# RWKV attention and a squared-ReLU MLP: the four w_in loads on ScalarE's DMA queue

## The chip, the cores and the metric

The kernel runs on one core of one Trainium2 chip. The core has TensorE (PE, with the weight load PEld beside it), VectorE (DVE), ScalarE (ACT), GpSimd (POOL) and SyncE (SP), and 16 DMA engines that move what the queues of the issuing engines hand them. The metric is the device time of one execution in microseconds (us); lower is better. In three runs the kernel took 182.17, 182.38 and 182.93 us, a median of 182.38 us.

## The reference

The first half is a linear attention with a decaying state (RWKV-6), for 4 batches, 8 heads, 768 tokens and 48 values per head. The second half is an MLP over the 3072 tokens, from 384 to 2048 values and back, with a squared ReLU between. All inputs and the output are float32.

```python
for t in range(S):                       # per batch b and head h
    cur = outer(u * k[t], v[t])
    y[t] = r[t] @ (state + cur)
    state = w[t][:, None] * state + outer(k[t], v[t])
x = y laid out as (4 * 768, 8 * 48)
h = maximum(x @ w_in, 0.0)               # w_in: 384 x 2048
out = (h * h) @ w_out                    # w_out: 2048 x 384
```

## The kernel before

The 3072 tokens are cut into 12 steps of 256 tokens, three steps to a batch. Each step has an attention part and an MLP part. Inside a step the tokens stand in two chunks of 128 rows.

The attention part of step s loads w, k, r and v (384 KB each: 128 partitions, 8 heads, two neighbouring tokens of 48 floats, so 384 bytes in one piece). POOL or DVE multiplies pairs of w (`ww_`), ACT takes the logarithm (`lw_`), PE sums it along the tokens (`cum_`), ACT takes the exponential (`exp_`, and `ac_` for the decay of a whole chunk). POOL makes the products of k and w (`kw_`, line 290), of r and w (`rw_`, line 286) and of k and u (`ku_`, `qp_`). DVE multiplies r and k by the decay (`rd_.s.0` makes rdec, line 358; `rd_.s.1` makes kdec, line 361). PE transposes both (`tr_`), and ACT or DVE copies the transposes out of PSUM (`rkt_`). PE makes the products of r and k (`p_`, line 420), the update of the state (`su_`, from v and kdec), the two parts of y (`y_`, `yc_`), and transposes y (`yt_`). ACT casts v (`v_`, and `vs_` in another order of rows). `vq_` (POOL or DVE, line 316) is the part of the token itself, which DVE adds to y (`ysb_`).

The MLP part runs in groups. `m1_.s.g` is one group of the first product (line 536), followed by the ReLU on ACT or DVE (`rl_`) and the square (`sq_`). `m2_` is the second product (line 561), `os_` scales it and `store` writes it out. Group g of `m1_` covers columns 256 g to 256 g + 255 of w_in, so it needs block g // 2 of four.

The weights are loaded once. Each of the four blocks of w_in (128 x 3 x 512 floats, 768 KB, pieces of 2 KB) is loaded into one of four staging buffers (`w_st`, `load_wi`) and cast to bf16 (`cast.i.g`, line 200). The four blocks of w_out (`load_wo`, `cast.o.g`) then use the same four staging buffers, so a w_out load waits for a cast of w_in. Blocks 1 and 0 of w_in are cast by ACT, 2 and 3 by POOL.

The order of the work is not left to a scheduler. The string ORDER lists all operations, and each engine does its own in this order; a letter behind `=` names the engine of an operation that can stand on several (A for ACT, V for DVE, G for POOL). All loads, stores and DMA transposes are issued by SP, also in this order. The entries `warm_.n.b` are n products of zeros on PE whose result nobody uses. Before the first m1, PE has step 0 and most of steps 1 and 2 of the attention in its order; the first m1 groups are 3 and 2 (block 1), then 1 and 0 (block 0), then 5 and 4 (block 2).

SP issues, at the start: w, k, r, u of step 0, w 1, v 0, k 1, r 1, w 2, v 1, r 2, k 2, then w_in blocks 1, 0 and 2, v 2, w_in block 3, w_out block 0, w 3, and so on. Eight completion semaphores are used in turn, so a DMA also waits, before it is issued, for the one eight places ahead of it.

Of the kernel before, what the change touches and what calls it, by code (L numbers as in the profile page):

```python
# [27 lines left out]
m1_.0.5:0 v_.2=A xt_.1=V qp_.2=G sn_.1.1 m1_.0.4:1 rl_.0.5=A p_.2.1:1 su_.2:b sq_.0.0=A rl_.0.4=V ld.2.o
m1_.1.4:0 cast.i.3=G ts_.2.0=V pm_.2.1 m1_.1.5:1 rl_.1.4=A q_.2 sn_.2.0 m1_.1.3:0 rl_.1.5=A ld.3.o vs_.2.1=G
vs_.2.0=A yc_.2.0:0 yc_.2.1:0 rl_.1.3=V m1_.1.6:1 cast.o.0=G qs_.2=A m1_.1.0:0 ld.3.k rl_.1.6=V sq_.0.2=A  # L30
y_.2:0 rl_.1.0=V m1_.1.1:1 vq_.2=G m1_.1.7:0 rl_.1.1=V ld.3.v m2_.0.1.0:0 sq_.1.2=A rl_.1.7=V sq_.0.1=A
cast.o.1=G m1_.1.2:1 rl_.1.2=A ysb_.2=V m1_.0.7:0 ld.4.w ww_.3=G yt_.2:1 rl_.0.7=V m1_.0.6:1 xt_.2=V m2_.0.1.1
sq_.1.1=A rl_.0.6=V ld.5.w m1_.2.6:0 cast.o.2=G lw_.3 sq_.1.0=A rl_.2.6=A cum_.3:1 sq_.1.3=A rw_.3=G al_.3
ld.5.r m2_.0.0.0:1 m1_.2.7:1 m2_.0.0.1 cast.o.3=V exp_.3 sq_.0.3=A ld.4.k rd_.3.0 kw_.3=G m1_.2.1:0 rl_.2.7=A
ac_.3 m2_.0.1.2 m2_.0.0.2 rl_.2.1=V ku_.3=G m2_.0.0.3 rd_.3.1 ld.4.v m2_.0.1.3 vs_.3.0=A m1_.2.0:1 os_.0.1=V
qp_.3=G ld.5.v m1_.2.3:0 os_.0.0=V rl_.2.0=V tr_.3.1:0 rl_.2.3=A tr_.3.0:1 rkt_.3.1=V v_.3=A ld.4.r m1_.2.4:1
ww_.4=G rkt_.3.0=V m2_.1.0.0:0 rl_.2.4=A q_.3 ww_.5=G p_.3.1:0 vs_.3.1=A ld.6.k su_.3:1 pm_.3.1 p_.3.0:m
m2_.1.0.1 ts_.3.0=A lw_.4 sn_.3.0 ld.5.k pm_.3.0 m2_.1.0.2 qs_.3=A m2_.1.1.0:1 sq_.2.0=A vq_.3=G ts_.3.1=V
m2_.1.0.3 ld.6.w cum_.4:0 m2_.1.1.1 ku_.4=G ac_.4 al_.4 store.0.1 m1_.2.5:0 os_.1.0=A v_.5=A yc_.3.1:1 y_.3:1
lw_.5 kw_.4=G m1_.2.2:1 ld.6.r ysb_.3=V rl_.2.5=A m2_.1.1.2 exp_.4 sn_.3.1 rl_.2.2=V yt_.3:0 rw_.4=G cum_.5:1  # L40
xt_.3=V m2_.1.1.3 vs_.4.0=A ac_.5 sq_.2.1=A qp_.4=G al_.5 m1_.3.0:0 rd_.4.1 v_.4=A m1_.3.3:1 rd_.4.0 dtr_.4.1
m2_.2.0.0:0 rl_.3.0=A rw_.5=G rl_.3.3=A m2_.2.0.1 os_.1.1=V exp_.5 q_.4 dtr_.4.0 su_.4:0 sq_.2.2=A m1_.3.4:0
kw_.5=G rd_.5.0 ww_.6=G m2_.2.1.0:1 rl_.3.4=A ts_.4.0=V sq_.2.3=A m1_.3.5:1 vs_.4.1=A rd_.5.1 sn_.4.0
m2_.2.1.1 store.1.0 ts_.4.1=V rl_.3.5=V ku_.5=G m1_.3.6:0 store.1.1 m2_.2.1.2 qs_.4=A ld.7.w ld.6.v rw_.6=G
p_.4.1:1 rl_.3.6=A p_.4.0:0 pm_.4.1 pm_.4.0 m2_.2.1.3 lw_.6 vq_.4=G m1_.3.1:1 m1_.3.2:0 rl_.3.1=A su_.5:1
dtr_.5.1 dtr_.5.0 vs_.5.1=G sq_.3.0=A rl_.3.2=V yc_.4.0:0 yc_.4.1:0 sn_.4.1 y_.4:0 os_.2.1=V sq_.3.1=A
m1_.3.7:1 ysb_.4=V ld.7.v m2_.2.0.2 rl_.3.7=A ld.8.w kw_.6=G vs_.5.0=G yt_.4:1 ld.7.k sq_.3.3=A m2_.2.0.3
xt_.4=V cum_.6:0 al_.6 m1_.4.4:0 qp_.5=G os_.2.0=A ac_.6 m1_.4.7:1 ts_.5.0=V exp_.6 rl_.4.4=V m2_.3.0.0:1
rl_.4.7=A rd_.6.1 m1_.4.6:0 rd_.6.0 m2_.3.0.1 dtr_.6.1 m2_.3.1.0:0 ku_.6=G qp_.6=G sq_.3.2=A rl_.4.6=A q_.5
dtr_.6.0 p_.5.0:1 p_.5.1:0 vs_.6.0=A m1_.4.5:1 sn_.5.0 m2_.3.0.2 qs_.5=G rl_.4.5=A pm_.5.1 pm_.5.0 vq_.5=G  # L50
m1_.4.1:0 m1_.4.3:1 rl_.4.3=A store.2.1 ld.8.v m2_.3.0.3 rl_.4.1=V ld.8.k v_.6=A ww_.7=G y_.5:0 q_.6 os_.3.0=A
ld.7.r m1_.4.0:1 store.0.0 ld.9.k ww_.8=G yc_.5.0:0 qs_.6=A su_.6:1 yc_.5.1:0 ysb_.5=V vs_.6.1=A ts_.6.0=V
m1_.4.2:0 ld.8.r m2_.3.1.1 rl_.4.0=V yt_.5:1 xt_.5=V sn_.6.0 lw_.7 vq_.6=G rl_.4.2=A p_.6.0:0 m2_.3.1.2
sq_.4.3=A store.2.0 pm_.6.0 m1_.5.2:1 ku_.7=G m1_.5.6:0 ts_.6.1=V yc_.6.1:0 sq_.4.0=A rl_.5.2=A p_.6.1:1
rl_.5.6=A m2_.3.1.3 kw_.7=G pm_.6.1 sq_.4.2=A m1_.5.4:1 rw_.7=G m1_.5.3:0 os_.3.1=V rl_.5.4=A y_.6:0 sn_.6.1
rl_.5.3=A cum_.7:1 kw_.8=G ysb_.6=V al_.7 m2_.4.0.0:1 vs_.7.1=A m1_.5.7:1 m1_.5.5:0 v_.7=G dyt_.6 sq_.4.1=A
rl_.5.7=V qp_.7=G rl_.5.5=V m2_.4.1.0:0 exp_.7 ld.9.w ld.9.v m2_.4.0.1 ac_.7 rd_.7.0 sq_.5.1=A m2_.4.0.2
ku_.8=G rd_.7.1 sq_.5.3=A dtr_.7.0 m2_.4.0.3 m1_.5.0:1 lw_.8 m1_.5.1:0 rw_.8=G rl_.5.0=V su_.7:0 q_.7
rl_.5.1=A cum_.8:1 dtr_.7.1 m1_.6.3:1 qs_.7=A m1_.6.5:0 rl_.6.3=V ld.10.w qp_.8=G ac_.8 sq_.5.0=A m2_.4.1.1
os_.4.0=V ts_.7.0=V ld.11.w sn_.7.0 m1_.6.4:1 rl_.6.5=A al_.8 ww_.9=G m2_.4.1.2 ld.9.r rl_.6.4=V exp_.8  # L60
store.3.0 m2_.5.1.0:1 sq_.5.2=A rd_.8.1 ts_.7.1=V sn_.7.1 m1_.6.0:0 vs_.7.0=G vs_.9.1=A rd_.8.0 m2_.4.1.3
m2_.5.1.1 kw_.9=G rl_.6.0=A dtr_.8.0 p_.7.1:0 v_.8=A p_.7.0:1 vq_.7=G pm_.7.1 m1_.6.1:1 m2_.5.1.2 rl_.6.1=A
pm_.7.0 ku_.9=G m2_.5.1.3 sq_.6.0=A lw_.9 m1_.6.6:0 dtr_.8.1 store.3.1 q_.8 yc_.7.0:0 v_.9=A yc_.7.1:0
rl_.6.6=V rw_.9=G su_.8:1 y_.7:0 os_.5.1=A ts_.8.0=V m1_.6.2:1 ysb_.7=V os_.4.1=A cum_.9:1 m1_.6.7:0 al_.9
dyt_.7 m2_.5.0.0:1 rl_.6.2=V exp_.9 ww_.10=G rl_.6.7=V m2_.5.0.1 ac_.9 ld.10.r rd_.9.1 sq_.6.1=A sq_.6.2=A
sn_.8.0 qp_.9=G ld.10.k qs_.8=G store.4.1 m2_.5.0.2 ld.10.v rd_.9.0 m2_.5.0.3 m2_.6.1.0:0 vs_.8.1=G sq_.6.3=A
dtr_.9.0 vs_.8.0=A p_.8.0:m p_.8.1:0 pm_.8.0 su_.9:1 m2_.6.1.1 ts_.9.0=A pm_.8.1 m2_.6.1.2 lw_.10 m1_.7.4:0
rw_.10=G os_.5.0=V m1_.7.0:1 rl_.7.4=V sn_.9.0 vq_.8=G yc_.8.1:0 dtr_.9.1 yc_.8.0:0 rl_.7.0=V y_.8:0 m1_.7.1:0
q_.9 rl_.7.1=A ts_.9.1=V m2_.6.1.3 kw_.10=G ysb_.8=V m1_.7.7:1 sq_.7.0=A ww_.11=G cum_.10:1 dyt_.8 rl_.7.7=V
m1_.7.5:0 qs_.9=A al_.10 m2_.6.0.0:1 v_.10=G rl_.7.5=A m1_.7.2:1 exp_.10 ld.11.k vs_.9.0=G m2_.6.0.1 lw_.11  # L70
rd_.10.0 rd_.10.1 m1_.7.3:0 rl_.7.2=A vq_.9=G ac_.10 m2_.6.0.2 os_.6.1=A rl_.7.3=A vs_.10.0=A store.6.1
m1_.7.6:1 store.5.1 ku_.10=G m2_.6.0.3 vs_.10.1=A ld.11.r sn_.9.1 rl_.7.6=V m1_.8.5:0 dtr_.10.0 p_.9.1:0
rl_.8.5=A p_.9.0:1 qp_.10=G pm_.9.1 m1_.8.3:1 m2_.7.0.0:0 rl_.8.3=A pm_.9.0 m1_.8.4:0 sq_.7.1=A m1_.8.2:1
os_.6.0=A y_.9:0 sq_.7.3=A rl_.8.2=V yc_.9.1:0 rw_.11=G su_.10:1 m2_.7.1.0:1 sq_.7.2=A ts_.10.0=V ysb_.9=V
m2_.7.1.1 rl_.8.4=A ku_.11=G q_.10 m1_.8.7:1 dyt_.9 m1_.8.1:0 rl_.8.7=V cum_.11:0 dtr_.10.1 kw_.11=G sn_.10.0
rl_.8.1=A m2_.7.1.2 al_.11 m1_.8.0:1 exp_.11 ld.11.v qs_.10=G ts_.10.1=V sn_.10.1 vq_.10=G m1_.8.6:0 rl_.8.0=A
store.6.0 rd_.11.0 m2_.7.1.3 rl_.8.6=A rd_.11.1 m1_.9.4:1 sq_.8.0=A ac_.11 dtr_.11.0 m1_.9.1:0 qp_.11=G
rl_.9.4=V sq_.8.2=A m2_.7.0.1 os_.7.1=V p_.10.1:1 sq_.8.1=A p_.10.0:0 pm_.10.1 store.5.0 dtr_.11.1 store.7.1
m1_.9.0:1 v_.11=G pm_.10.0 vs_.11.1=G m2_.8.1.0:1 rl_.9.0=A rl_.9.1=A m2_.8.1.1 sq_.8.3=V m1_.9.5:1 m2_.7.0.2
m2_.7.0.3 os_.7.0=A yc_.10.0:1 yc_.10.1:1 rl_.9.5=V su_.11:0 y_.10:1 m1_.9.2:0 ysb_.10=V m1_.9.6:1 rl_.9.2=A  # L80
ts_.11.0=V dyt_.10 m2_.8.0.0:0 rl_.9.6=V sn_.11.0 m1_.9.3:0 q_.11 m2_.8.1.2 rl_.9.3=A yc_.11.0:1 vs_.11.0=A
p_.11.1:0 yc_.11.1:1 p_.11.0:m m2_.8.0.1 pm_.11.0 m2_.8.0.2 pm_.11.1 sq_.9.1=A m2_.8.0.3 m2_.8.1.3 qs_.11=A
# [549 lines left out]
```

## Time and profile before

| What | Value |
|---|---|
| Runs | 182.17, 182.38, 182.93 us |
| Span of the profiled execution | 182.2 us |
| PE busy | 171.8 us (94%) |
| DVE, ACT, POOL busy | 130.0, 132.7, 122.7 us |
| Loads of w_in | 4 of 768 KB, median 11.1 us from issue to landing |
| Loads of w, k, r, v | 48 of 384 KB, medians 5.3 to 5.9 us |
| Hardware DMA queue | 79184 packets, 35.46 MB |

The page gives the profiled execution by its span alone, from the first to the last instruction; the runs are the device's own time, and their median lies 0.2 us above that span.

How to read it: busy times of engines run beside each other and do not add up. A row of the timeline has the start in us, the time it took, the engine, the line, the operation, the tile written, the tile read and the count; brackets give the idle time of the engine before it and what ended that. SPq is SP as it issues DMAs: the time in such a row is the issue, and the data land later. The DMA rows give that second time, from issue to landing.

### The profile page before, as it was taken

The numbers are of one execution on the slowest core, as the hardware profiler recorded it, in microseconds if no ns is written. First come the engines' busy times: TensorE is split into PE (matmuls) and PEld (weight loads), VectorE is DVE, ScalarE is ACT, GpSimd is POOL, SyncE is SP. The second block draws the span as 40 slices with busy tenths as digits, with TensorE's granted clock in tenths as the row PEclk, the third lists the DMA queues.
The fourth block names the chain that finished last, engine by engine and source line by source line (L and its number), as shares of the span: only waits on it lengthen the run. The fifth ranks groups of instructions, "written<-read, shape, count | busy, mean of one in ns | idle before, by whom it ended". The sixth has DMA issues, their size and how long they took to land.

```text
span 182.2 us, 5695 instructions
## 1 busy us (share of the span) xinstructions
PE 171.8 (94%) x2385; PEld 123.4 (68%) x2385; DVE 130.0 (71%) x195; ACT 132.7 (73%) x235; POOL 122.7 (67%) x140
## 2 busy tenths in 40 slices
...
DMA packets 79208, 35.81 MB, mean 197 GB/s; under 512 B 72400, under 2 KB 77648, under 8 KB 79184
## 3 DMA queue, kind: packets, MB, share of 16 engines
q1 hardware_dynamic: 79184, 35.46, 85.9%
...
## 4 chain that ended last, share of the span: by engine, by line
PE 75%; SPq 10%; DMA 8%; ACT 4%; issue 1%; DVE 1%; ACTq 0%
PE bk L561 32%; PE m L536 32%; SPq L178 8%; DMA w_st<-in_moe_w_in_dram 5%; PE att L420 3%; DMA rT<-rdec_buf 2%; PE att L483 2%; PE att L493 2%; PE att L446 1%; ACT gt L545 1%; PE att L326 1%; ACT wi_sb L200 1%; PE bk L516 1%; SPq L188 1%; SPq L205 1%
## 5 line engine op out<-in xcount | busy, mean ns | idle before, releaser
L536 PE MATMUL m<-xT,wi_sb 128*128 128x256 bf16 x576 | 74.0, 273 | 1.3 <-ACT gt L545 1.2
L561 PE MATMUL bk<-wo_sb,gt 128*128 128x384 bf16 x384 | 71.9, 326 | 0.0
L536 PEld LDWEIGHTS <-wi_sb 128*128 128x128 bf16 x576 | 54.8, 98 | 13.0 <-issue 0.9
L561 PEld LDWEIGHTS <-gt 128*128 128x128 bf16 x384 | 36.9, 98 | 19.2
L545 ACT ACTIVATE gt<-m 128x512 f16<-128x512 f32 x56 | 33.0, 595 | 22.3 <-PE m L536 21.9
L553 ACT ACTIVATE gt<-gt 128x1024 bf16<-128x1024 f16 x42 | 43.3, 1051 | 1.4 <-DVE gt L547 1.1
L547 DVE TENSOR_SCALAR gt<-m 128x512 f16<-128x512 f32 x40 | 27.0, 686 | 9.6 <-PE m L536 9.3
L434 DVE TENSOR_TENSOR pmT<-att,mask 128x1024 bf16<-128x1024 f32 x20 | 23.9, 1218 | 4.5 <-PE att L420 4.5
L297 POOL TENSOR_TENSOR ku<-k_raw,u_bc 128x768 f32<-128x768 f32 x12 | 21.8, 1819 | 0.2 <-DMA u_bc<-in_u_dram 0.2
L302 POOL TENSOR_TENSOR ku<-ku,r_raw 128x768 f32<-128x768 f32 x11 | 20.7, 1881 | 0.2
L316 POOL TENSOR_TENSOR ku<-v_sh,qs 128x768 f32<-128x768 bf16 x11 | 16.3, 1479 | 4.9 <-ACT qs L277 4.8
L277 ACT CAST v_sh<-v_raw 64x384 bf16<-64x384 f32 x34 | 17.3, 508 | 0.4
L290 POOL TENSOR_TENSOR k_raw<-k_raw,w_raw 128x384 f32<-128x384 f32 x12 | 12.2, 1013 | 6.4 <-DMA k_raw<-in_k_dram 6.3
L286 POOL TENSOR_TENSOR r_raw<-r_raw,w_raw 128x384 f32<-128x384 f32 x12 | 12.0, 1000 | 6.4 <-DMA r_raw<-in_r_dram 6.4
L504 DVE TENSOR_TENSOR y_sb<-att,ku 128x768 bf16<-128x768 f32 x12 | 11.4, 953 | 5.5 <-issue 1.6
L461 POOL TENSOR_TENSOR S<-t_state,ac_buf 128x192 bf16<-128x192 f32 x20 | 10.2, 512 | 6.4 <-DVE t_state L456 3.4
L361 DVE TENSOR_TENSOR kdec_buf<-k_raw,att 128x768 bf16<-128x768 f32 x12 | 11.4, 949 | 3.4 <-ACT att L340 2.8
L358 DVE TENSOR_TENSOR rdec_buf<-r_raw,att 128x384 bf16<-128x384 f32 x24 | 12.1, 547 | 2.2 <-ACT att L340 1.1
L340 ACT ACTIVATE att<-att 128x768 f32<-128x768 f32 x12 | 9.6, 798 | 3.1 <-PE att L328 1.9
L568 ACT ACTIVATE o_sb<-bk 128x384 f32<-128x384 f32 x13 | 6.3, 485 | 7.4 <-PE bk L561 7.3
L307 DVE TENSOR_REDUCE q<-ku 128x16 f32<-128x768 f32 x12 | 11.3, 943 | 0.0
L578 PE MATMUL att<-warm 128*128 128x512 bf16 x27 | 9.1, 492 | 1.2 <-DVE half_ones L228 1.2
...
## 6 DMA issues: line engine op xcount, KB each, us to landing
w_raw<-in_w_dram SPq DMA_DIRECT2D x12, 384.0 KB, 5.3
k_raw<-in_k_dram SPq DMA_DIRECT2D x12, 384.0 KB, 5.9
r_raw<-in_r_dram SPq DMA_DIRECT2D x12, 384.0 KB, 5.7
v_raw<-in_v_dram SPq DMA_DIRECT2D x12, 384.0 KB, 5.8
...
w_st<-in_moe_w_in_dram SPq DMA_DIRECT2D x4, 768.0 KB, 11.1
w_st<-in_moe_w_out_dram SPq DMA_DIRECT2D x4, 768.0 KB, 9.3
rT<-rdec_buf SPq DMA_TRANSPOSE x16, 4.1
```

The costliest lines, as they stand in the source:

```text
L178: nc.sync.dma_start(out=t[:, hs, at:at + 2, :].rearrange("p h j d -> p h (j d)"), in_=src[b, hs, i * T:(i + 1) * T, :].rearrange("h (p j) ...
L277: copy(out[j * Q:(j + 1) * Q, c], src[c * Q:(c + 1) * Q, :, j])
L290: tensor_mul("kw_", s, h)(raw["k", s][:, hs, 0, :], raw["k", s][:, hs, 1, :], raw["w", s][:, hs, 1, :])
L297: tensor_mul("ku_", s, h)(tiles["ku", s][:, hs], raw["k", s][:, hs, 1:3, :], u_bc[:, hs, None, :].to_broadcast([C, n, 2, D]))
L302: tensor_mul("qp_", s, h)(ku, ku, raw["r", s][:, heads(h), 0:2, :])
L316: tensor_mul("vq_", s)(vq[:], tiles["vs", s][:], tiles["qs", s][:, :, :, None].to_broadcast([C, 2, H, D]))
L434: nc.vector.tensor_mul(pmT, ps_p[:].rearrange("p e (x t) -> p (e x) t", t=C), mk.to_broadcast([C, 8, C]))
L536: nc.tensor.matmul(ps1[:, j, :], wi_sb[:, n // 4, kk, n % 4 * 128:(n % 4 + 1) * 128], tiles["xT", s][:, :, kk, :], start=(kk == 0), stop=( ...
L545: nc.scalar.activation(rl, m1, AF.Relu, scale=RS)
L547: nc.vector.tensor_scalar(out=rl, in0=m1, scalar1=RS, scalar2=0.0, op0=ALU.mult, op1=ALU.max)
L553: nc.scalar.activation(gt, rl, AF.Square)
L561: nc.tensor.matmul(m2, gt[:, n, c * C:(c + 1) * C], wo_sb[:, n, :], start=(n == 0), stop=(n == NT - 1))
```

## The change

The four `ld.g.i` entries move in ORDER and get an engine. Blocks 1 and 0 are issued by ACT behind `exp_.0`, blocks 2 and 3 by ACT behind `rkt_.0.0`, so all four in the first step. Before, they stood on SP behind k of step 2. A helper `queue` picks the issuing engine; the w_out loads go through it too, but have no engine in ORDER and stay on SP. Nothing else changes in the order of any engine: SP has the same list without the four. In the new file, lines behind ORDER are two higher (286 becomes 288, 536 becomes 538).

```diff
-ld.0.w ld.0.k ld.0.r ld.0.u ld.1.w ww_.0=V lw_.0 warm_.11.5 cum_.0:0 kw_.0=G exp_.0 rd_.0.1 ld.0.v warm_.8.5
+ld.0.w ld.0.k ld.0.r ld.0.u ld.1.w ww_.0=V lw_.0 warm_.11.5 cum_.0:0 kw_.0=G exp_.0 ld.1.i=A ld.0.i=A rd_.0.1
...
-rkt_.0.0=A qp_.0=V ld.2.r v_.0=A warm_.5.5 p_.0.0:m p_.0.1:1 ac_.0 lw_.1 q_.0 su_.0:b ld.2.k cum_.1:0
+ww_.1=V rkt_.0.0=A ld.2.i=A ld.3.i=A qp_.0=V ld.2.r v_.0=A warm_.5.5 p_.0.0:m p_.0.1:1 ac_.0 lw_.1 q_.0 su_.0:b
...
-ts_.0.0=A kw_.1=G pm_.0.0 pm_.0.1 vs_.0.0=A sn_.0.0 ld.1.i exp_.1 rw_.1=G vs_.0.1=A qs_.0=A rd_.1.1 ku_.1=G
-warm_.3.2 yc_.0.1:1 ld.0.i ac_.1 ts_.0.1=V rd_.1.0 warm_.2.2 tr_.1.1:0 sn_.0.1 y_.0:1 rkt_.1.1=A vq_.0=V
-tr_.1.0:1 ww_.2=G ld.2.i v_.1=A rkt_.1.0=V ysb_.0=V vs_.1.1=A warm_.4.2 p_.1.1:0 qp_.1=G su_.1:m ld.2.v
-pm_.1.1 lw_.2 yt_.0:0 cum_.2:1 ld.3.i ts_.1.0=V rw_.2=G q_.1 exp_.2 kw_.2=G xt_.0=V vs_.1.0=A rd_.2.0 qs_.1=G
...
+    def queue(*op):
+        return nc.scalar if where[op] == "A" else nc.sync
+
...
     def load_wi(g):
         w_st["i", g] = stage_pool.tile([C, KT, GW], FP32, name="w_st")
-        nc.sync.dma_start(
+        queue("ld", g, "i").dma_start(
             out=w_st["i", g][:],
             in_=moe_w_in[:, g * GW:(g + 1) * GW].rearrange("(a p) f -> p a f", p=128))
 
     def load_wo(g):
         w_st["o", g] = stage_pool.tile([C, 4, DM], FP32, name="w_st")
-        nc.sync.dma_start(
+        queue("ld", g, "o").dma_start(
```

In the program as built, the first w_out load takes the staging buffer of w_in block 2 and waits for POOL's cast of it; before the change it took the buffer of block 1 and waited for ACT's cast. The waits that the four loads have on ACT are: none for block 1, w of step 0 for block 0, u for block 2, and v of step 0 for block 3.

More of the change, by code (lines that the diff above doesn't have):

```diff
@@ L28 @@
[L28 to L82, printed above, removed]
@@ new lines @@
+yt_.0:0 cum_.2:1 ts_.1.0=V rw_.2=G q_.1 exp_.2 kw_.2=G xt_.0=V vs_.1.0=A rd_.2.0 qs_.1=G ac_.2 cast.i.1=A
+rd_.2.1 warm_.10.1 tr_.2.0:1 sn_.1.0 p_.1.0:0 ku_.2=G ts_.1.1=V yc_.1.1:1 tr_.2.1:0 cast.i.0=A pm_.1.0 ld.0.o
+m1_.0.3:0 ld.3.w rkt_.2.1=V m1_.0.2:1 vq_.1=G rkt_.2.0=V y_.1:1 rl_.0.3=A yc_.1.0:1 rl_.0.2=V p_.2.0:0 m1_.0.1:0
+ld.1.o ysb_.1=V cast.i.2=G m1_.0.0:1 rl_.0.1=A pm_.2.0 yt_.1:0 ld.3.r rl_.0.0=A m1_.0.5:0 v_.2=A xt_.1=V qp_.2=G
+sn_.1.1 m1_.0.4:1 rl_.0.5=A p_.2.1:1 su_.2:b sq_.0.0=A rl_.0.4=V ld.2.o m1_.1.4:0 cast.i.3=G ts_.2.0=V pm_.2.1
@@ new lines @@
+m1_.1.5:1 rl_.1.4=A q_.2 sn_.2.0 m1_.1.3:0 rl_.1.5=A ld.3.o vs_.2.1=G vs_.2.0=A yc_.2.0:0 yc_.2.1:0 rl_.1.3=V
+m1_.1.6:1 cast.o.0=G qs_.2=A m1_.1.0:0 ld.3.k rl_.1.6=V sq_.0.2=A y_.2:0 rl_.1.0=V m1_.1.1:1 vq_.2=G m1_.1.7:0
+rl_.1.1=V ld.3.v m2_.0.1.0:0 sq_.1.2=A rl_.1.7=V sq_.0.1=A cast.o.1=G m1_.1.2:1 rl_.1.2=A ysb_.2=V m1_.0.7:0
+ld.4.w ww_.3=G yt_.2:1 rl_.0.7=V m1_.0.6:1 xt_.2=V m2_.0.1.1 sq_.1.1=A rl_.0.6=V ld.5.w m1_.2.6:0 cast.o.2=G
+lw_.3 sq_.1.0=A rl_.2.6=A cum_.3:1 sq_.1.3=A rw_.3=G al_.3 ld.5.r m2_.0.0.0:1 m1_.2.7:1 m2_.0.0.1 cast.o.3=V
@@ new lines @@
+exp_.3 sq_.0.3=A ld.4.k rd_.3.0 kw_.3=G m1_.2.1:0 rl_.2.7=A ac_.3 m2_.0.1.2 m2_.0.0.2 rl_.2.1=V ku_.3=G
+m2_.0.0.3 rd_.3.1 ld.4.v m2_.0.1.3 vs_.3.0=A m1_.2.0:1 os_.0.1=V qp_.3=G ld.5.v m1_.2.3:0 os_.0.0=V rl_.2.0=V
+tr_.3.1:0 rl_.2.3=A tr_.3.0:1 rkt_.3.1=V v_.3=A ld.4.r m1_.2.4:1 ww_.4=G rkt_.3.0=V m2_.1.0.0:0 rl_.2.4=A q_.3
+ww_.5=G p_.3.1:0 vs_.3.1=A ld.6.k su_.3:1 pm_.3.1 p_.3.0:m m2_.1.0.1 ts_.3.0=A lw_.4 sn_.3.0 ld.5.k pm_.3.0
+m2_.1.0.2 qs_.3=A m2_.1.1.0:1 sq_.2.0=A vq_.3=G ts_.3.1=V m2_.1.0.3 ld.6.w cum_.4:0 m2_.1.1.1 ku_.4=G ac_.4
```

71 lines of the change are left out of this document (57 added, 14 removed).

## The prediction

> **What bounds the kernel now.** I read the windows view first: the share of each engine in stretches of the span, the granted clock, then the mean load of the 16 DMA engines (over 1 where packets overlap) and GB/s.
>
> ```profile
> core 0: us, PE busy (x) PEld busy (x) DVE busy (x) ACT busy (x) POOL busy (x), PEclk, DMA share, GB/s
> 8.00:12.00 4.00, 3.98 (x60) 2.26 (x59) 3.33 (x6) 2.27 (x3) 2.38 (x2) 1.00 1.23 275
> 12.00:16.00 4.00, 2.64 (x74) 1.21 (x62) 4.00 (x5) 3.90 (x9) 2.65 (x4) 1.00 1.28 264
> 16.00:20.00 4.00, 2.78 (x37) 1.81 (x37) 3.17 (x6) 2.86 (x9) 4.00 (x4) 1.00 0.95 217
> 24.00:27.00 3.00, 2.29 (x51) 1.43 (x50) 2.64 (x5) 1.68 (x3) 2.84 (x6) 1.00 1.03 373
> 36.00:46.00 10.00, 10.00 (x132) 8.17 (x131) 7.86 (x12) 9.56 (x17) 8.96 (x9) 1.00 1.06 307
> 46.00:176.00 130.00, 129.37 (x1810) 95.72 (x1808) 94.08 (x140) 99.00 (x177) 87.33 (x94) 1.00 0.83 170
> ```
>
> There are two stages. From 36 to 176 us PE is busy for 139.4 of 140 us: its order is written out, so what is late at 36 us is late by as much at the end. Before that, PE waits, and the DMA engines are full: the step inputs, in short packets, move at 264 to 275 GB/s, and the first weights, in long ones, at 373.
>
> Second, the timeline of SP, the only queue that loads (start, time to issue), and the DMA view, narrowed to one issue at a time (KB, us from issue to landing):
>
> ```profile
> 0.74 0.46 SPq L178 DMA_DIRECT2D w_raw<-in_w_dram  x1
> ...
> 4.80 1.15 SPq L178 DMA_DIRECT2D v_raw<-in_v_dram  x1
> 5.99 2.64 SPq L178 DMA_DIRECT2D k_raw<-in_k_dram  x1
> 14.62 2.92 SPq L178 DMA_DIRECT2D k_raw<-in_k_dram  x1
> 17.59 2.40 SPq L188 DMA_DIRECT2D w_st<-in_moe_w_in_dram  x3
> 20.55 3.36 SPq L188 DMA_DIRECT2D w_st<-in_moe_w_in_dram  x1
> 26.74 1.27 SPq L194 DMA_DIRECT2D w_st<-in_moe_w_out_dram  x1
> ```
>
> ```profile
> k_raw<-in_k_dram SPq DMA_DIRECT2D x1, 384.0 KB, 7.2
> k_raw<-in_k_dram SPq DMA_DIRECT2D x1, 384.0 KB, 7.1
> w_st<-in_moe_w_in_dram SPq DMA_DIRECT2D x1, 768.0 KB, 7.6
> w_st<-in_moe_w_in_dram SPq DMA_DIRECT2D x1, 768.0 KB, 13.6
> ```
>
> In order: k of step 1 lands at 5.99 + 7.2 = 13.2 us, k of step 2 at 14.62 + 7.1 = 21.7, the first w_in block at 17.59 + 7.6 = 25.2, the last at 20.55 + 13.6 = 34.2. Short packets first, weights behind them. The page's count of packets gives the sizes:
>
> ```profile
> DMA packets 79208, 35.81 MB, mean 197 GB/s; under 512 B 72400, under 2 KB 77648, under 8 KB 79184
> ```
>
> The 79184 - 77648 = 1536 longest are the w_in blocks (3.15 MB in all, so 2 KB each); a step input goes by 384 B, one head's pair of rows.
>
> Third, the timelines of the engines around the start of the first MLP product, m1 (start, us, in brackets the idle time before and what ended it). POOL, ACT, DVE, then PE:
>
> ```profile
> 13.35 1.02 POOL L290 TENSOR_TENSOR k_raw<-k_raw,w_raw 128x384 f32<-128x384 f32 x1 [2.75 <-DMA k_raw<-in_k_dram]
> 22.40 1.00 POOL L290 TENSOR_TENSOR k_raw<-k_raw,w_raw 128x384 f32<-128x384 f32 x1
> 26.79 1.48 POOL L316 TENSOR_TENSOR ku<-v_sh,qs 128x768 f32<-128x768 bf16 x1
> 30.67 1.46 POOL L200 CAST wi_sb<-w_st 128x1536 bf16<-128x1536 f32 x1 [2.40 <-DMA w_st<-in_moe_w_in_dram]
> 37.43 1.47 POOL L200 CAST wo_sb<-w_st 128x1536 bf16<-128x1536 f32 x1
> ```
>
> ```profile
> 6.84 0.80 ACT L340 ACTIVATE att<-att 128x768 f32<-128x768 f32 x1 [1.10 <-PE att L328]
> 9.40 1.01 ACT L392 COPY kT<-bk 128x1024 bf16<-128x1024 bf16 x1 [1.76 <-PE bk L374]
> 10.49 1.01 ACT L389 COPY rT<-bk 128x1024 bf16<-128x1024 bf16 x1
> 11.75 0.83 ACT L272 CAST v_bf<-v_raw 128x768 bf16<-128x768 f32 x1 [0.25 <-DMA v_raw<-in_v_dram]
> 28.55 1.47 ACT L200 CAST wi_sb<-w_st 128x1536 bf16<-128x1536 f32 x1 [1.84 <-DMA w_st<-in_moe_w_in_dram]
> ```
>
> ```profile
> 25.28 0.95 DVE L361 TENSOR_TENSOR kdec_buf<-k_raw,att 128x768 bf16<-128x768 f32 x1 [0.36 <-POOL S L461]
> ```
>
> ```profile
> 11.78 0.43 PE L420 MATMUL att<-rT,kT 64*64 64x128 bf16 x16
> 12.63 0.44 PE L446 MATMUL bk<-v_bf,kdec_buf 64*64 64x48 bf16 x32 [0.43 <-ACT v_bf L272]
> 26.54 0.62 PE L374 MATMUL bk<-ident,kdec_buf 128*128 128x128 bf16 x8
> 26.99 1.47 PE L536 MATMUL m<-xT,wi_sb 128*128 128x256 bf16 x12
> 28.94 0.40 PE L420 MATMUL att<-rT,kT 64*64 64x128 bf16 x16
> 30.57 1.47 PE L536 MATMUL m<-xT,wi_sb 128*128 128x256 bf16 x12 [1.23 <-ACT gt L545]
> 32.21 1.47 PE L536 MATMUL m<-xT,wi_sb 128*128 128x256 bf16 x12
> ```
>
> Weights do arrive late: POOL idles 2.40 us for block 2, ACT 1.84 us for block 0, and through ACT's relu behind that cast PE idles 1.23 us. That is all an earlier weight can win. But the m1 at 26.99 stands on PE behind the transposes of step 2's decayed k (26.54), which need kdec (25.28), k of step 2 and POOL's kw_2 (22.40, just 0.7 us after the landing). POOL itself is the tight one there: 4.00 of the 4 us from 16 to 20 us.
>
> **The change part by part.**
>
> Removed from SP: four issues, 2.40 + 3.36 us. They stood behind every step-2 input but v, so SP gains nothing ahead of k of step 2. The later loads could move up, but see the fourth part.
>
> Added to ACT: blocks 1 and 0 behind exp_0 (ends 7.64), blocks 2 and 3 behind the copy at 10.49 (ends 11.50). ACT has no row for an issue. SP's go from 0.46 us (the first one, ring empty) to 3.36 (ring full); three w_in blocks took 2.40, and I take that, 0.8 each, as ACT's ring is empty and the blocks are the same. Then the first two, 1.6 us, fit into the 1.76 us of idle time before 9.40. The other two stand ahead of v_0, ac_0, lw_1, ts_0 and the rest of step 0 on ACT; the last waits for v of step 0, as v_0 does, and that input will be late, which covers them. Cost 0; without that cover 1.6 us. At 0.46 each nothing changes; four times 3.36 less the 1.76 would make step 0 late by 11.7 us on ACT, which is more than the shift found next: the far end above. The program's waits of the other three (on w, none, on u of step 0) are met when ACT gets there, u perhaps just so.
>
> Moved ahead in the DMA engines: this is what counts. Four times 768 KB are 3.15 MB; at 373 GB/s that is 8.4 us. They are issued from 7.7 us on, when w and everything later of step 1, v of step 0 and all of step 2 but v (until 21.7 us) have still to come. If all four are served before k of step 2, it lands 8.4 us later; 0.7 us I give back for the hole in 16 to 20 us ((264 - 217) x 4 / 264), which a second ring could fill. So 21.7 + 8.4 - 0.7 = 29.4 us.
> The Trainium skill, DMA: Bandwidth & Descriptors, "Issuing engines are not separate DMA queues", says that transfers from every issuing engine end on the same 16 engines and interleave, so that only issue time is saved. The load near 1 in the rows agrees; were it otherwise, with a ring of its own capacity, the sum would be the gain of 1.2 us below.
>
> What follows: kw_2 starts at 29.5 instead of 22.40, +7.1 us. The POOL work from there to the cast of block 2 (qs_1, a state, ku_2, vq_1; 22.40 to 28.27) keeps its length; the 2.40 us wait goes, as the weights lie ready. The cast comes at 29.5 + 5.9 = 35.4 us, and its m1, at 32.21 right behind the cast's end (32.13), at 36.9: +4.7 us. On PE the same: kdec (about 1 us) and the transposes (26.54 to 26.99) follow kw_2's end (30.5), the first m1 is at 32.1 (+5.1); p_2's end is 2.35 us behind it (29.34 - 26.99), so the m1 of 30.57 comes at 34.5 (+3.9), its own 1.23 us wait gone. POOL is the later of the two: +4.7.
>
> A changed buffer: in the built program the first w_out load takes the staging buffer of block 2, cast by POOL, where before it took that of block 1, cast by ACT. It is issued at the cast's end, about 36.9 instead of 26.74, with w of step 3 and everything later behind it on SP. Its own cast ran at 37.43 and is now wanted near 42.1. With the engines then empty of step inputs, 768 KB need 2.1 us at 373 GB/s, or 7.6 by the quickest long row: 39 to 44.5 us. I take nothing, since the engines start empty; +2.4 us is the upper end.
>
> Sum on the profiled execution: span 182.2 + 4.7 = 186.9; runs before have a median 0.2 us above that span, so 187.1 us.
>
> **The rivals.**
> - Two rings move more than one. If short and long packets together reached 373 GB/s, then from about 9.2 us (issue plus latency) 12.5 us of step inputs at 264, 3.3 MB, and 3.15 MB of weights take 17.3 us: k of step 2 at 26.5. kw_2 is 4.2 us late, less 2.4: +1.8, 184.2 us. For it: long packets alone do reach that rate. Against: short ones have a load of 1.28 on their own, so they lack engine time and not requests.
> - The clock of PE falls. If v of step 0 is late, PE stands between 12.2 us (end of 11.78) and v_0. A long packet per short one from each ring would hold v for almost the 6.3 us of three blocks: PE is idle for over 5 us.
>
> ```profile
> 1.19 4.87 PE L578 MATMUL att<-warm 128*128 128x512 bf16 x11 [1.19 <-DVE half_ones L228]
> 22.11 2.32 PE L578 MATMUL bk<-warm 128*128 128x512 bf16 x10
> ```
>
> Early dummy matmuls took 443 ns each (4.87/11), later ones 232. At the slow rate the ten ahead of tr_2 take 2.1 us more, on PE's path to m1: 189.2 us. The Trainium skill, TensorE: Matmul & The Clock Gate, "Part 1: The HAM clock gate", has the clock halve after an idle window of about 3.4 us; the slow first rows fit, but no long gap in this trace tests it. Against: w and v are 2.5 us from landed at 9.2 (11.7 now); if the rings share evenly that becomes 5, v_0 ends at 15 and the gap is about 3 us.
> - It gets faster. If SP's ring is served first, or ACT's trickles, the step inputs keep their times and the weights still come before 25 us: PE's 1.23 us wait goes, 181.2 us. It decides at k of step 2: 0.7 us of slack ahead of kw_2 plus 2.4 ahead of the cast let it be 3.1 us late at no loss. So the weights may get no more than 3.1/8.4, some 37%, of their bytes in before it. For it: SP has a head start of several issues. Against: ACT's packets are 2 KB, the others 384 B, so an even turn by packet gives ACT most of the bytes; and the first w_out load, now behind a cast that ends near 29.7, would take part of it back.
> - Near that point (a share around 35 to 45%) gain and loss cancel: 182.4.
>
> The Trainium skill, DMA: Bandwidth & Descriptors, "Queues, rings and completion order", has each DMA engine take turns between rings by packet, which would rule out the third rival; no row here has two loading rings, so the trace can't tell.
>
> **How the numbers follow.** Forecast (185.3 to 188.2) 0.57; two rings faster (183.4 to 185.3) 0.14; clock falls (above 188.2, with slow issues on ACT) 0.14; cancels 0.08; faster 0.07. The range reaches from 183.3, where k of step 2 is about 25.9, to 189.5, the clock's price on top; it leaves out the two last cases and the far end of the clock's, under 0.2. A change of 0.5% (0.9 us) is about what can be told from none: faster 0.07, same 0.08, slower 0.85.
>
> **What would show it.** ACT's four issues at about 7.7 and 11.5 us, none much over 1 us; v of step 0 cast well after 11.75; k of step 2 landing near 29 and POOL's third L290 row (two lines lower in the new file) waiting on that DMA; no wait ahead of any w_in cast; m1 first at 32, then PE full at the same pace; the first w_out issue behind POOL's cast. Wrong if that POOL row stays near 22 to 25 us, or if PE regains the time after 36 us; if PE's dummy rows near 30 us take over 400 ns, the second rival holds.

## The result and the profile after

The changed kernel takes 192.39 us (median of five runs, 191.88 to 193.91); the kernel before, run beside it, takes 182.38 (five runs, 181.97 to 183.09). The ratio is 1.0559 with an interval of 1.0525 to 1.0593: slower by 10.0 us. The direction was forecast; the time lies 2.9 us above the range. Profiled span against profiled span it is 192.1 - 182.2 = 9.9 us, and these 9.9 us are accounted for below. The ratios in this text leave out two executions that ran slow as a whole, one of 191.56 us among the runs of the early place on SP's queue and one of 186.85 us among those of the last experiment. (With each run's span now known, the time of an execution lies 1.8 us above its span, 193.91 against 192.1, so the shown execution of before took some 184.0 us and not the median. Both shown executions are about 1.5 us above their medians, so the difference is not touched.)

First the windows view of the kernel after (per stretch: busy time of each engine and count, granted clock, DMA load, GB/s):

```profile
core 0: us, PE busy (x) PEld busy (x) DVE busy (x) ACT busy (x) POOL busy (x), PEclk, DMA share, GB/s
12.00:16.00 4.00, 1.90 (x56) 0.99 (x45) 2.97 (x4) 3.78 (x9) 0.00 (x0) 1.00 1.07 360
16.00:20.00 4.00, 0.00 (x0) 0.00 (x0) 0.00 (x0) 1.27 (x5) 0.00 (x0) 0.61 1.07 360
20.00:24.00 4.00, 1.61 (x23) 1.01 (x23) 1.22 (x2) 0.18 (x1) 1.46 (x2) 0.50 1.21 273
...
28.00:32.00 4.00, 4.00 (x68) 2.53 (x67) 3.73 (x6) 2.50 (x5) 4.00 (x4) 0.68 0.52 136
32.00:36.00 4.00, 3.38 (x58) 2.11 (x56) 3.64 (x7) 3.13 (x5) 3.80 (x8) 1.00 0.00 0
```

From 12 to 20 us more bytes move than before (360 GB/s against 264 and 217), and yet POOL, busy for 6.65 of these 8 us before, does nothing, and PE nothing from 16 to 20. Later, from 32 to 36 us, the DMA engines stand empty, where before they moved 336 GB/s. The bytes moved are the wrong ones, as the DMA view of 12 to 18 us shows (packets by size; then by queue, q1 SP's and q10 ACT's, the packets, the MB and the share of the 16 engines' time):

```profile
DMA packets 1830, 2.16 MB, mean 360 GB/s; under 512 B 952, under 2 KB 952, under 8 KB 1829
...
q10 hardware_dynamic: 920, 1.80, 84.1%
q1 hardware_dynamic: 909, 0.35, 21.9%
```

In these 6 us 920 packets of ACT's queue and 909 of SP's were served: nearly one for one. Of ACT's, 952 - 909 = 43 are under 512 B and the other 877 are the 2 KB pieces of the weights; SP's have 384 B. So the step inputs get 0.35 of 2.15 MB, 16%. SP's stream falls to 0.35 MB / 6 us = 58 GB/s, where it had 264 alone. Just before, it was worse: from 11 to 12 us the same view has 189 packets of ACT's queue and 9 of SP's.

The timelines of the two queues (start, time to issue), and the DMA view's times to landing, one issue at a time, for k and r of step 1 and k of step 2:

```profile
6.85 0.80 ACT L342 ACTIVATE att<-att 128x768 f32<-128x768 f32 x1 [1.11 <-PE att L330]
6.86 0.96 ACTq L190 DMA_DIRECT2D w_st<-in_moe_w_in_dram  x2
...
10.50 1.57 ACTq L190 DMA_DIRECT2D w_st<-in_moe_w_in_dram  x2
12.12 0.83 ACT L274 CAST v_bf<-v_raw 128x768 bf16<-128x768 f32 x1 [0.61 <-DMA v_raw<-in_v_dram]
```

```profile
6.05 2.12 SPq L180 DMA_DIRECT2D k_raw<-in_k_dram  x1
8.21 1.75 SPq L180 DMA_DIRECT2D r_raw<-in_r_dram  x1
...
12.82 8.74 SPq L180 DMA_DIRECT2D v_raw<-in_v_dram  x1
...
24.28 1.27 SPq L180 DMA_DIRECT2D k_raw<-in_k_dram  x1
...
39.10 0.37 SPq L196 DMA_DIRECT2D w_st<-in_moe_w_out_dram  x1
```

```profile
k_raw<-in_k_dram SPq DMA_DIRECT2D x1, 384.0 KB, 14.7
r_raw<-in_r_dram SPq DMA_DIRECT2D x1, 384.0 KB, 16.2
k_raw<-in_k_dram SPq DMA_DIRECT2D x1, 384.0 KB, 5.5
```

k of step 1 lands at 6.05 + 14.7 = 20.8 us (13.2 before), r of step 1 at 8.21 + 16.2 = 24.4 (14.8 before), k of step 2 at 24.28 + 5.5 = 29.8 (21.7 before). Now the timelines of POOL and of PE around the first m1:

```profile
20.87 1.00 POOL L292 TENSOR_TENSOR k_raw<-k_raw,w_raw 128x384 f32<-128x384 f32 x1 [10.55 <-DMA k_raw<-in_k_dram]
...
24.46 1.00 POOL L288 TENSOR_TENSOR r_raw<-r_raw,w_raw 128x384 f32<-128x384 f32 x1 [2.12 <-DMA r_raw<-in_r_dram]
...
32.06 1.01 POOL L292 TENSOR_TENSOR k_raw<-k_raw,w_raw 128x384 f32<-128x384 f32 x1
...
37.62 1.46 POOL L202 CAST wi_sb<-w_st 128x1536 bf16<-128x1536 f32 x1
...
52.25 1.46 POOL L202 CAST wo_sb<-w_st 128x1536 bf16<-128x1536 f32 x1 [2.47 <-DMA w_st<-in_moe_w_out_dram]
```

```profile
22.39 0.42 PE L495 MATMUL att<-S,rT 64*64 64x48 bf16 x16 [7.64 <-POOL S L463]
...
35.58 1.47 PE L538 MATMUL m<-xT,wi_sb 128*128 128x256 bf16 x12
...
37.85 1.48 PE L538 MATMUL m<-xT,wi_sb 128*128 128x256 bf16 x12
...
39.51 1.47 PE L538 MATMUL m<-xT,wi_sb 128*128 128x256 bf16 x12
```

This is where the time goes. Before, rw_1 was this row:

```profile
14.81 1.00 POOL L286 TENSOR_TENSOR r_raw<-r_raw,w_raw 128x384 f32<-128x384 f32 x1
```

Now it is the row at 24.46: +9.65. From there POOL has no gap in either kernel until kw_2, and it takes 22.40 - 14.81 = 7.59 us before and 32.06 - 24.46 = 7.60 after. (That the two agree so well is in part chance: among the rows between, one product took 1.80 us instead of 2.55 and a state 1.22 instead of 0.52.) So kw_2 is 9.66 us later, and not because of k of step 2, which was there 2.3 us earlier. The first m1 is 8.6 us later; the wait of 1.23 us ahead of the second is gone, and the m1 of block 2 stands 39.51 - 32.21 = 7.3 us later. POOL's cast of that block, 6.95 us later and without a wait, ends at 39.08, just ahead of it; PE has no gap from 37.85 on, so here PE's own line is the later of the two by some 0.4 us. The chain of waits (start, length, what it was) says the same, and names the second part:

```profile
8.21 16.18 DMA r_raw<-in_r_dram
...
24.46 1.00 POOL r_raw L288
...
44.32 10.08 DMA w_st<-in_moe_w_out_dram
```

The first w_out load is issued at 39.10 us, where it was at 26.74. The third and fourth are then late for their casts (POOL's at 52.25 waits 2.47 us), and step 3's inputs behind them. PE, busy for 129.37 of the 130 us from 46 us on before, is short of work again (the windows view):

```profile
56.00:80.00 24.00, 22.28 (x317) 15.56 (x316) 18.42 (x30) 19.48 (x40) 21.84 (x19) 1.00 0.98 224
```

This and the 5 us behind it bring PE's shift from 7.3 us to 9.85, at the m1 that before starts at 74.9; at the end it is 9.9.

### The profile page after: what moved, and what is told of

It is laid out like the page before. It is cut to its first block, busy times and chain, and to the rows that moved or that the text cites. A ratio compares the mean times of both kernels' runs of the same rounds, so it can differ in the third digit from the quotient of the medians.

```text
span 192.1 us, 5694 instructions
## 1 busy us (share of the span) xinstructions
PE 175.0 (91%) x2385; PEld 125.4 (65%) x2385; DVE 130.1 (68%) x195; ACT 132.8 (69%) x235; POOL 122.3 (64%) x140
## 3 DMA queue, kind: packets, MB, share of 16 engines
q10 hardware_dynamic: 1600, 3.15, 4.6%
## 4 chain that ended last, share of the span: by engine, by line
PE 46%; DMA 23%; POOL 11%; DVE 6%; SPq 6%; issue 3%; ACT 3%; DVEq 0%; POOLq 0%; ACTq 0%
PE bk L563 21%; PE m L538 19%; DMA r_raw<-in_r_dram 11%; DMA w_st<-in_moe_w_out_dram 5%; SPq L180 5%; DMA v_raw<-in_v_dram 4%; DMA rT<-rdec_buf 3%; PE att L422 2%; POOL ku L304 2%; POOL ku L299 2%; POOL S L463 2%; POOL r_raw L288 2%; POOL ku L318 1%; DVE rdec_buf L360 1%; PE att L485 1%
## 5 line engine op out<-in xcount | busy, mean ns | idle before, releaser
L304 POOL TENSOR_TENSOR ku<-ku,r_raw 128x768 f32<-128x768 f32 x11 | 20.0, 1815 | 0.2
L318 POOL TENSOR_TENSOR ku<-v_sh,qs 128x768 f32<-128x768 bf16 x11 | 16.2, 1474 | 4.9 <-ACT qs L279 4.7
L463 POOL TENSOR_TENSOR S<-t_state,ac_buf 128x192 bf16<-128x192 f32 x20 | 10.9, 544 | 7.1 <-DVE t_state L458 5.0
L495 PE MATMUL att<-S,rT 64*64 64x48 bf16 x320 | 5.4, 191 | 8.0 <-POOL S L463 7.6
```

The costliest lines, as they stand in the source:

```text
L304: tensor_mul("qp_", s, h)(ku, ku, raw["r", s][:, heads(h), 0:2, :])
L318: tensor_mul("vq_", s)(vq[:], tiles["vs", s][:], tiles["qs", s][:, :, :, None].to_broadcast([C, 2, H, D]))
L463: nc.gpsimd.tensor_mul(t[:], tiles.pop(("ts", s, c))[:].rearrange("p (a d) -> p a d", a=HP), tiles["a_c", s][:, :, c, None].to_broadcast([ ...
```

## The experiments

Four things were changed together: the place of the issues in time, the queue, the staging buffers, and (through PE's holes) the clock. The main theory was that packets of a second queue overtake the step inputs. Its rivals: that the early place alone does it, on whatever queue; that the staging buffers do; that the clock does. The kernel before took 183.44 us beside the first four runs below, and 182.69 us beside the other four; differences are against these. The times of the first four lie 0.8 to 1.0 us above the ranges expected of them; as differences from the kernel before, which itself took 1.1 us more there than beside the change (182.38), they lie inside.

**The early place, on SP's queue** (against the change):

```diff
-... kw_.0=G exp_.0 ld.1.i=A ld.0.i=A rd_.0.1
+... kw_.0=G exp_.0 ld.1.i ld.0.i rd_.0.1
...
-ww_.1=V rkt_.0.0=A ld.2.i=A ld.3.i=A qp_.0=V ld.2.r
+ww_.1=V rkt_.0.0=A ld.2.i ld.3.i qp_.0=V ld.2.r
```

> The four loads keep the early places of the change but go back to SP's queue, so the order is one line and no packet can overtake. Turns (two rings alternate packet by packet, so long packets overtake the inputs of step 1): r of step 1 is then late only by the first two blocks, 1.57 MB at 373 GB/s = 4.2 us instead of 9.65; k of step 2 by all four, near 29.5 us as in the change. POOL's kw_2 is near 30 instead of 32.06, and the end 2 us or more ahead of the change: 188.5 us (187 to 190). Bytes alone (only what stands ahead of k of step 2 counts): the same as the change, 192.4. Clock (the halved PE clock is what costs): PE still stands over 4 us for v of step 0, so the clock falls as well: 191 to 192.4.

190.90 us in the median of all four executions; by the ratio, 1.037 (1.0283 to 1.0458), +6.8. The profile is of the longest of the four, 191.56 us (the shortest took 188.56). POOL's and PE's timelines:

```profile
19.04 1.01 POOL L288 TENSOR_TENSOR r_raw<-r_raw,w_raw 128x384 f32<-128x384 f32 x1
...
30.15 1.01 POOL L292 TENSOR_TENSOR k_raw<-k_raw,w_raw 128x384 f32<-128x384 f32 x1 [0.33 <-DMA k_raw<-in_k_dram]
...
35.70 1.46 POOL L202 CAST wi_sb<-w_st 128x1536 bf16<-128x1536 f32 x1
```

```profile
33.78 2.77 PE L538 MATMUL m<-xT,wi_sb 128*128 128x256 bf16 x12
...
37.91 1.62 PE L538 MATMUL m<-xT,wi_sb 128*128 128x256 bf16 x12
```

Here rw_1 is only 4.2 us late, which is what the two blocks now ahead of step 1's inputs would take (1.57 MB at 373 GB/s), and step 2's inputs decide, as the prediction had it: cast of block 2 at 35.70 (the prediction's working gave 35.4), +5.0. But PE's m1 runs at half pace, 2.77 us in place of 1.47, and the second one is 7.3 us late; what that pace cost the other three executions is not shown. The first w_out load goes out at 32.06 us, at the end of ACT's first cast, so the buffers are those of before too. An early place thus costs time on either queue; what the queue does, the next run tells.

**The queue, at the old places in ORDER** (against before, with `queue` as in the change; the staging tiles are written out so that each load takes the buffer it had before):

```diff
-... sn_.0.0 ld.1.i exp_.1
+... sn_.0.0 ld.1.i=A exp_.1
...
-warm_.3.2 yc_.0.1:1 ld.0.i ac_.1
+warm_.3.2 yc_.0.1:1 ld.0.i=A ac_.1
...
-tr_.1.0:1 ww_.2=G ld.2.i v_.1=A
+tr_.1.0:1 ww_.2=G ld.2.i=A v_.1=A
...
-pm_.1.1 lw_.2 yt_.0:0 cum_.2:1 ld.3.i ts_.1.0=V
+pm_.1.1 lw_.2 yt_.0:0 cum_.2:1 ld.3.i=A ts_.1.0=V
...
-        w_st["i", g] = stage_pool.tile([C, KT, GW], FP32, name="w_st")
+        w_st["i", g] = stage[(1, 0, 2, 3).index(g)][:].rearrange("p (a f) -> p a f", a=KT)
...
-        w_st["o", g] = stage_pool.tile([C, 4, DM], FP32, name="w_st")
+        w_st["o", g] = stage[g][:].rearrange("p (a d) -> p a d", a=4)
```

> The four loads keep the late places of the kernel before in the order of the work, but go by ACT's queue; staging buffers as before. Turns: ACT gets to the first at 14.3 us and the rest at 17 to 21.5 us, ahead of SP's 17.6, and its long packets overtake v of step 1 and r and k of step 2, which land near 27, 29 and 30 us instead of 19.1, 20.4 and 21.7; the first m1 near 34 to 35 us; 188 to 190 us. Place alone (the queue does not matter, only that the loads came early): within 1 us of before, 182 to 183.4.

190.91 us, 1.0402 (1.035 to 1.0454): +7.5, with the place and the buffers of before. ACT reaches the four entries at 12.95, 15.44, 16.65 and 19.16 us, while SP still works through its inputs (it reached them at 17.59 and 20.55 us). POOL, then PE:

```profile
14.61 1.00 POOL L289 TENSOR_TENSOR r_raw<-r_raw,w_raw 128x384 f32<-128x384 f32 x1
...
26.66 1.00 POOL L289 TENSOR_TENSOR r_raw<-r_raw,w_raw 128x384 f32<-128x384 f32 x1 [5.35 <-DMA r_raw<-in_r_dram]
30.04 1.01 POOL L293 TENSOR_TENSOR k_raw<-k_raw,w_raw 128x384 f32<-128x384 f32 x1 [2.38 <-DMA k_raw<-in_k_dram]
...
35.59 1.46 POOL L203 CAST wi_sb<-w_st 128x1536 bf16<-128x1536 f32 x1
```

```profile
27.29 0.23 PE L377 MATMUL bk<-ident,rdec_buf 128*128 128x128 bf16 x1 [2.89 <-DVE rdec_buf L361]
...
32.49 0.42 PE L496 MATMUL att<-S,rT 64*64 64x48 bf16 x16 [3.27 <-POOL S L464]
...
33.67 2.77 PE L539 MATMUL m<-xT,wi_sb 128*128 128x256 bf16 x12
...
37.33 1.48 PE L539 MATMUL m<-xT,wi_sb 128*128 128x256 bf16 x12
```

Step 1 is untouched (14.61 against 14.81), step 2's r and k are overtaken: kw_2 at 30.04 and the cast of block 2 at 35.59, +4.9. Again the m1 runs at half pace behind two holes of about 3 us. The queue is cause enough, with no earlier place in ORDER: through it the loads go out earlier in time, and share the DMA engines with what SP has issued (from 21 to 26 us 766 packets of ACT's queue against 732 of SP's).

**Half of it** (against before, `queue` and the buffers as in the last; blocks 2 and 3 stay on SP at their old places):

```diff
-... kw_.0=G exp_.0 rd_.0.1 ld.0.v warm_.8.5
+... kw_.0=G exp_.0 ld.1.i=A ld.0.i=A rd_.0.1 ld.0.v warm_.8.5
...
-... sn_.0.0 ld.1.i exp_.1
+... sn_.0.0 exp_.1
-warm_.3.2 yc_.0.1:1 ld.0.i ac_.1
+warm_.3.2 yc_.0.1:1 ac_.1
```

> Only blocks 1 and 0 go early by ACT; 2 and 3 stay on SP at their old places; staging buffers as before. Turns: 48 long packets on each DMA engine, each with one short packet, take near 5.1 us in which SP's stream moves what it moves in 1.15 us alone: everything of SP behind that is 3.9 us late. r of step 1 at POOL near 18.7 us, k of step 2 near 25.6, the first m1 near 31 instead of 26.99, the m1 of 30.57 near 33.2; 185.1 us (184.2 to 186.2). If the cost came from the waits of blocks 2 and 3 on ACT or from the changed staging buffer alone, this is at 182.4 or below.

187.03 us, 1.0204 (1.0158 to 1.025): +3.6, over a third of the change's. POOL's rows:

```profile
20.38 1.00 POOL L289 TENSOR_TENSOR r_raw<-r_raw,w_raw 128x384 f32<-128x384 f32 x1 [1.22 <-DMA r_raw<-in_r_dram]
...
27.98 1.00 POOL L293 TENSOR_TENSOR k_raw<-k_raw,w_raw 128x384 f32<-128x384 f32 x1
...
33.53 1.48 POOL L203 CAST wi_sb<-w_st 128x1536 bf16<-128x1536 f32 x1
```

r of step 1 decides (its row was expected at 18.7 us), and from it to kw_2 lie 27.98 - 20.38 = 7.60 us again. With the runs so far, one sum gives the cast of block 2: kw_2 starts at rw_1 + 7.6 us or when k of step 2 is in, whichever is later, and the cast stands 5.55 us behind it.

| Kernel | rw_1 | rw_1 + 7.6 | kw_2 | cast of block 2, less kw_2 |
|---|---|---|---|---|
| before | 14.81 | 22.41 | 22.40 | 8.27 (2.40 of it waiting for the block) |
| the change | 24.46 | 32.06 | 32.06 | 5.56 |
| half of it | 20.38 | 27.98 | 27.98 | 5.55 |
| early on SP | 19.04 | 26.64 | 30.15, waits for k of step 2 | 5.55 |
| ACT, old places | 14.61 | 22.21 | 30.04, waits for k of step 2 | 5.55 |

**The staging buffers** (the change, with the buffers of before):

```diff
-        w_st["i", g] = stage_pool.tile([C, KT, GW], FP32, name="w_st")
+        w_st["i", g] = stage[(1, 0, 2, 3).index(g)][:].rearrange("p (a f) -> p a f", a=KT)
...
-        w_st["o", g] = stage_pool.tile([C, 4, DM], FP32, name="w_st")
+        w_st["o", g] = stage[g][:].rearrange("p (a d) -> p a d", a=4)
```

> The change with the staging buffers of before: the first w_out load goes into the buffer of w_in block 1, cast by ACT (end near 35.1 and 36.5 us for two blocks), and not into that of block 2, cast by POOL (end 39.1). If the late w_out loads, and the 9 us in which the DMA engines move next to nothing, make the last 2.6 us of the 9.9 (the shift of PE is 7.3 us at the second pair of m1 groups and 9.9 at the end): 189 to 190.5 us, PE's shift staying near 7.3. If those 2.6 us have another cause (the phase of the DMA transposes, the clock): 192.4 as the change.

191.46 us, 1.0437 (1.0378 to 1.0495): +8.0. The first w_out load goes out at 34.94 us instead of 39.10, and PE is full in the later stretch:

```profile
56.00:78.00 22.00, 22.00 (x324) 16.03 (x322) 17.56 (x29) 18.38 (x39) 18.49 (x17) 1.00 0.91 211
```

PE's shift is 7.1 us at the m1 that before starts at 30.57, still 7.1 at the one that starts at 116.7, and 7.8 at the end; in the change it was 7.3 at the first and 9.7 at the second. The early place on SP's queue, with the old buffers as well, shows no late growth either (7.3 and 7.1 us). So the changed buffer makes the late part of the loss.

**The change once more**, beside the runs that follow, with no edit:

> The change once more, beside the other three on the same chip: 10 us behind the kernel before (5.3 to 5.9%), as first measured.

192.42 us, 1.0525 (1.048 to 1.057): +9.7. The shift is 7.4 us at the m1 of 30.57, and 8.9 at that of 116.7 and at the end. Up to there the changed buffers thus cost 1.5 us here and 2.4 in the first profile, and the old ones nothing; the price is known to that. The times alone do not show it: the intervals, 1.0378 to 1.0495 and 1.048 to 1.057, touch.

**The clock, in the change** (31 more dummy products where PE stands):

```diff
-ku_.1=G warm_.3.2 yc_.0.1:1 ac_.1
+ku_.1=G warm_.34.2 yc_.0.1:1 ac_.1
```

> The change with 34 dummy matmuls instead of 3 in the hole that PE has at 14.7 to 22.4 us, so that its clock stays up. Turns (POOL's row of work from r of step 1 on sets the first m1, and PE only follows it): within 0.7 us of the change. Clock (the half clock from 16.9 to 30.6 us is on the path): 1.5 to 3 us faster than the change.

192.13 us, 1.0521 (1.0456 to 1.0586): no gain on 192.42. The clock stays up, and nothing moves (a window, then PE's first m1):

```profile
16.00:20.00 4.00, 4.00 (x21) 1.77 (x19) 0.00 (x0) 1.28 (x5) 0.00 (x0) 1.00 1.07 359
```

```profile
35.68 1.47 PE L538 MATMUL m<-xT,wi_sb 128*128 128x256 bf16 x12
```

In the change the clock does fall (0.61 and 0.50 above), but it is back before the first m1 (1.00 from 32 us), and what lies between waits for POOL. It costs nothing there.

**The clock, where step 2's inputs decide** (ACT at the old places, with dummy products in the two holes):

```diff
-ac_.2 cast.i.1=A rd_.2.1 warm_.10.1 tr_.2.0:1 sn_.1.0 p_.1.0:0 ku_.2=G
+ac_.2 cast.i.1=A rd_.2.1 warm_.20.1 tr_.2.0:1 sn_.1.0 p_.1.0:0 warm_.14.0 ku_.2=G
```

> The late places on ACT's queue, as in the earlier run of that name without warm, with 24 more dummy matmuls in PE's holes at 24.4 to 27.3 and 29.2 to 32.5 us. There the half clock fell on the first m1 groups (2.77 us for twelve matmuls against 1.47). If that half clock is on the path, 1.3 to 2 us are won on the 7.5 us that the late places cost: 5.5 to 6.2 us behind before. If POOL's cast of block 2 sets the end there too, no gain: 7.5 us behind.

```profile
33.01 1.47 PE L539 MATMUL m<-xT,wi_sb 128*128 128x256 bf16 x12
...
35.38 1.48 PE L539 MATMUL m<-xT,wi_sb 128*128 128x256 bf16 x12
```

In the profile PE's second m1 comes at 35.38 instead of 37.33 and the span is 187.3 instead of 189.0: there, by this one profile, the clock cost 1.7 us on the path. The medians do not settle it: 189.65 us, 1.038 (1.0309 to 1.0451), against 1.0402 for the same without the dummies. Two of its four runs kept the full clock (189.13 and 188.61), two did not (190.17 and 191.01 at 0.991, a clock that two executions of the kernel before show at 182.27 and 182.34 us).

**ACT's queue, behind the inputs** (against before, `queue` and the buffers of before; not the change's places):

```diff
-tr_.1.0:1 ww_.2=G ld.2.i v_.1=A rkt_.1.0=V ysb_.0=V vs_.1.1=A warm_.4.2
+tr_.1.0:1 ww_.2=G v_.1=A rkt_.1.0=V ysb_.0=V vs_.1.1=A ld.1.i=A ld.0.i=A warm_.4.2
...
-... rw_.2=G q_.1 exp_.2 kw_.2=G
+... rw_.2=G q_.1 exp_.2 ld.2.i=A ld.3.i=A kw_.2=G
```

> ACT's queue again, but behind the inputs of step 2: blocks 1 and 0 from about 21 us, 2 and 3 behind the exponential of step 2, near 23 us; staging buffers as before. Turns: nothing is left that they can overtake but v of step 2, so r and k of step 2 land near 20.4 and 21.7 as before and the time is that of before, within 1.5 us. If loads by ACT's queue cost by themselves (issue on ACT, two rings at once): 2 us or more behind before.

183.19 us, 1.0016 (0.999 to 1.0041): the same as before. POOL keeps its times, and PE's wait ahead of the second m1 is shorter by half:

```profile
14.88 1.00 POOL L289 TENSOR_TENSOR r_raw<-r_raw,w_raw 128x384 f32<-128x384 f32 x1
...
22.48 1.01 POOL L293 TENSOR_TENSOR k_raw<-k_raw,w_raw 128x384 f32<-128x384 f32 x1
...
30.02 1.46 POOL L203 CAST wi_sb<-w_st 128x1536 bf16<-128x1536 f32 x1 [1.68 <-DMA w_st<-in_moe_w_in_dram]
```

```profile
29.98 1.47 PE L539 MATMUL m<-xT,wi_sb 128*128 128x256 bf16 x12 [0.57 <-ACT gt L548]
```

So ACT's queue costs nothing by itself here; what costs is which packets go ahead of which. The 0.6 us won on that wait do not show in the medians, and no version tried beats the kernel before.

## Why the prediction was right and where it failed

- **What bounds the kernel**: right. What was late at 36 us stayed late to the end (the buffers, below, added to it), and no wait stands ahead of a w_in cast any more.
- **SP's four issues, and ACT's**: right in the sum, but not by the cover that was named. Taken one by one the issues have 0.38 to 0.50 us, not 0.8, and the first two lie beside the exponential. v of step 0, expected to be late, was not: it landed at 4.85 + 6.8 = 11.65 us. The fourth issue (0.38 us from 11.70) then stood ahead of its cast, which is at 12.12 instead of 11.75. These 0.4 us came to nothing, as POOL and PE next waited for step 1 until 20.87 and 22.39.
- **Weights ahead of k of step 2**: right, 29.8 us for a forecast of 29.4. The rival of the two rings moving more was half true: both together move 360 GB/s. It won nothing, as the added bytes are weights. The Trainium skill, DMA: Bandwidth & Descriptors, "Queues, rings and completion order", has a DMA engine take turns between rings by packet. The 920 packets against 909 from 12 to 18 us agree with that in number; the 189 against 9 from 11 to 12 us do not. The rival of a gain allowed some 37% of the weights' bytes ahead of k of step 2: they were all in at 11.70 + 11.8 = 23.5 us, ahead of its 29.8.
- **"kw_2 starts at 29.5 instead of 22.40"**: this step failed. It let only k of step 2 decide. If the weights go ahead of k of step 2 they also go ahead of k and r of step 1, which POOL needs 7.6 us earlier, and POOL had no gap between rw_1 and kw_2 to take that up (4.00 of 4 us busy, as the prediction itself quoted). kw_2 came at 32.06, 2.56 us after the forecast, and not waiting on k's DMA, the sign that the prediction had named. Of rw_1's 9.65 us, the turns explain an estimated 8.2: 3.15 MB at 1.80 MB / 6 us take 10.5 us, in which SP's stream moves (264 - 58) x 10.5 = 2.16 MB less, and these take 8.2 us at 264. The other 1.4 us are in the order: when r of step 1 was in, SP's queue had moved 3.69 MB (by 24.4 us), where before it had moved 3.32 MB (by 8.68 + 6.1 = 14.8 us). So 0.37 MB of later inputs went ahead of r's last packets, 1.4 us at 264 GB/s; why they did stays open.
- **What follows from kw_2**: right in form, the 2.40 us of waiting given back included. On POOL 5.56 us to the cast (5.9 forecast), on PE 2.5 us from kw_2's end to the first m1 (1.6 forecast; DVE's kdec, which was to start at kw_2's end, started 0.8 us behind it, released by POOL's next row). With kw_2 where it was, POOL's line comes to 7.0 us in place of 4.7, and PE's, which the prediction had as the earlier of the two, to 7.3.
- **"I take nothing, since the engines start empty"** for the changed buffer: the upper end named there, +2.4, was the nearer. It looked at the first w_out load alone, and that one was in time: it landed at 39.10 + 4.6 = 43.7 us, and its cast, at 44.36, did not wait. The third and fourth were late. The shift grew by 2.6 us to the end in the profile and by 1.5 in the repeat, and with the old buffers by 0.7, none of it where the new ones cost. The engines do start empty (0 GB/s from 32 to 36 us), but what they could have loaded in that time comes behind the cast, w_out blocks and step 3's inputs together, from 39.10 us on.
- **The sum**: 4.7 forecast, +2.3 on POOL's line for r of step 1, +0.3 as PE's line was the later one, +2.6 behind that, the buffers above all: 9.9.
- **The rival of the falling clock**: it happened, by another way (PE stood 7.64 us for POOL's state of step 1, not for v of step 0), and cost nothing in the change. Its sign, dummy rows over 400 ns near 30 us, was not there: the ten ahead of tr_2, at 30.82 us, took 2.32 us as before. Where the holes lie right ahead of the first m1 it is on the path in the profile, 1.7 us.
